# A spectral layer and an MLP in one kernel: x over the hardware queues, the first MLP block in two halves, the weight conversion on VectorE alone

## The chip, the cores and the metric

The kernel runs on one core of a Trainium2 chip. The metric is the device time of one execution in microseconds (us); the median of several runs counts. The core has a matrix engine (TensorE, PE in the profile, with its weight loads as PEld), VectorE (DVE), ScalarE (ACT), GpSimd (POOL) and SyncE (SP, which here only issues transfers). ACT, POOL and SP issue DMAs. Each engine works through its own instructions in order, and waits on semaphores for the others.

## The reference

```
X = rfft(x, axis=1)                       # x: 4 x 3008 x 256 float32
Yr = Xr @ w_r - Xi @ w_i + b_r
Yi = Xr @ w_i + Xi @ w_r + b_i
Y  = shrink(Yr, 0.01) + 1j * shrink(Yi, 0.01)     # sign(v) * max(|v| - 0.01, 0)
y  = irfft(Y, n=3008, axis=1)             # 4 x 3008 x 256
h  = y.reshape(12032, 256) @ moe_w_in     # moe_w_in: 256 x 2048, float64
out = (h * sigmoid(h)) @ moe_w_out        # moe_w_out: 2048 x 256, float64
```

## The kernel before, in words

The transform of length 3008 is done in two steps of products with tables, 47 x 64. For each of the four batches b, x is cut into eight groups g of 4 columns j (94 partitions x 1024 floats, 4 KB in a row).

- **s1** (one g): two products of 512 columns with table c1 into PSUM, a copy by ACT (tile s1o), and a store to a scratch tensor scr1 in DRAM.
- **The u loop**, twelve steps: u_load reads two rows of scr1 (tile a), **s2** multiplies with c2, ACT and DVE split the result into a high and a low part (xh, xl), **mix** multiplies with w_r and w_i in 24 products, DVE adds the bias and shrinks (y, three instructions), **split_z** makes zh and zl of y, **i1** multiplies with table c3 (tile t3) in six products, and ACT copies and stores the result to scr2.
- **i2**: reads scr2 (tile gin) and finishes the inverse transform for one block of 512 tokens, split into a high and a low part again (xt). i2_ends does the columns that cross a block's end.
- **The MLP**: 24 blocks of 512 tokens (the last has 256), 16 slices f of the hidden size each. One pair (block, f) is a **tick**: mlp1 (six products of 512 columns), sigmoid on ACT, the product g on DVE (L474), gh on ACT, gl on DVE (L484), and two ticks later mlp2 (per 128 tokens one product of 512 and one of 256 columns), which adds up in four PSUM banks (acc) over all 16 f.

A product of plain float32 runs as two passes on PE; a float32r one is one pass, and so three of them (high x high, high x low, low x high) stand for one exact product.

The weights of the MLP come as float64. Sixteen pieces (eight of w_in, eight of w_out; four for each quarter of f) are converted by w64_split: first an ACT instruction, then with one w_go the first half (L560, L561 on DVE), with the next w_go the second half (L566, L567 on DVE, L569 on ACT, L570 and L571 on POOL). w_begin loads the next piece and starts one.

The order is written out by hand: each engine's instructions stand in the order of the code. Ahead of the ticks (the prologue) come s1 of b = 0, the u loop of b = 0 with half a weight in most steps, s1 of b = 1, and i2 of block 0. From then on the list `ticks` sets the order, and `fill` says what stands behind mlp1 of which tick: i2 of the blocks ahead, weights (W_PLAN), and the transform of the other batches.

x loads go through POOL's queue (L149). b = 0's u loop takes its y split by POOL (L358). Loads and most stores go through SP, stores of scr2 in the u loop through ACT.

Of the kernel before, what the change touches and what calls it, by code (L numbers as in the profile page):

```python
# [21 lines left out]
NU = NR // 2  # L22
# [10 lines left out]
X_BUFS = [0, 1, 2, 3, 4, 5, 6, 0, 1, 2, 3, 4, 5, 2, 1, 0]  # L33
# [3 lines left out]
def dft_tables():  # L37
# [16 lines left out]
    for h in range(2):  # L54
# [33 lines left out]
    c3l = c3 - c3h  # L88
    return {
# [3 lines left out]
        "c4": c4.reshape(96, NP).astype(np.float32),  # L93
    }
# [3 lines left out]
def spectral_mlp_kernel(ctx: ExitStack, tc: tile.TileContext, x, w_r, w_i, b_r, b_i, w_in, w_out, c1, c2, c3, c4, out):  # L98
# [44 lines left out]
    def x_load(b, g):  # L143
        if b < 2:
            t = x_pre[X_BUFS[8 * b + g]]
        else:
            t = x_sb[g % 2]
        v = x[b].rearrange("(p j) d -> p (j d)", j=NJ)
        nc.gpsimd.dma_start(out=t[:NP, :], in_=v[:, g * 4 * D:(g + 1) * 4 * D])  # L149
        return t  # L150
# [15 lines left out]
    def s1(b, g, late=False):  # L166
        t = x_t.pop((b, g))
        if b == 1 and g > 4:
            o = x_pre[(4, 6, 2)[g - 5]][:96, :]
        else:  # L170
            tag, bufs = ("s1o", 2) if 8 * b + g in (6, 7, 10, 11, 12) else ("gin", 4)
            o = sb.tile([128, 4 * D], F32, tag=tag, bufs=bufs, name="s1o")[:96, :]
# [180 lines left out]
    def split_z(b, u):  # L353
# [135 lines left out]
    def mlp2(i, f):  # L489
        n = BLOCKS[i][1]  # L490
        gh, gl = gf.pop((i, f))
        for t in range(n // 128):
            if f == 0:
# [3 lines left out]
            if i == LAST:  # L497
# [8 lines left out]
                start=(f == 0), stop=False,  # L506
# [3 lines left out]
                start=False, stop=(f == NFF - 1),  # L510
# [36 lines left out]
    def w64_split(t, shape, hi, lo):  # L547
# [3 lines left out]
        def shaped(a):  # L551
# [10 lines left out]
                                       op0=ALU.bitwise_and, op1=ALU.bitwise_or)  # L562
        yield
# [5 lines left out]
        nc.scalar.copy(hi, w)  # L569
        nc.gpsimd.tensor_sub(w, w, hi)  # L570
        nc.gpsimd.tensor_tensor(out=lo, in0=w, in1=shaped(lw), op=ALU.add)  # L571

    with tc.manual_schedule():
# [72 lines left out]
        def u_step(b, u):  # L646
            if u < NU:
                if u + (3 if b == 0 else 2) < NU:
                    u_load(b, u + (3 if b == 0 else 2))
                s2(b, u)  # L650
            if u > 0:
                t3_load(b, u - 1)
            if b == 0:
                if u > 2:
                    w_go()
                if u % 2:
                    w_begin()
            if 0 <= u - 2 < NU:
                split_z(b, u - 2)
            if 0 <= u - 1 < NU:  # L660
                mix(b, u - 1)
            if 0 <= u - 3 < NU:
                i1(b, u - 3)
# [6 lines left out]
        w32 = [w_load(w_r), w_load(w_i)]  # L670
# [9 lines left out]
        for u in range(NU):  # L680
            u_step(0, u)
# [3 lines left out]
            if 1 < u < 8:  # L685
# [3 lines left out]
        split_z(0, NU - 2)  # L689
        t3_load(0, NU - 1)  # L690
        mix(0, NU - 1)
        i1(0, NU - 3)
        s1(1, 2)
        split_z(0, NU - 1)
        i1(0, NU - 2)
        w_tags[:] = [(("y", 2), ("i1o", 2)), (("zl", 2), ("zh", 2))]
        s1(1, 3, late=True)
# [4 lines left out]
        i2_load(0)
        flush(1)
        for g in (4, 5, 6, 7):
            s1(1, g, late=True)
            w_go()
            if g == 5:
                w_begin()
            if g > 5:
                w_go()  # L710
# [12 lines left out]
        taken = set(range(17, len(ticks), NFF))  # L723
# [9 lines left out]
        for i in range(1, len(BLOCKS)):  # L733
            at(16 * i - 9, i2_load, i)
            put(16 * i - 7, i2, i, 0)
            put(16 * i - 5, i2, i, 1)
            put(16 * i - 3, i2_ends, i)
        for t, (go, begin) in enumerate(W_PLAN):
            for _ in range(go):
                at(t, w_go)  # L740
            for _ in range(begin):
                at(t, w_begin)
        for t in (10, 11):
# [12 lines left out]
        for b, t0, dt in ((2, 30, 7), (3, 110, 8)):  # L756
# [49 lines left out]
```

## Time and profile before

| | us |
|---|---|
| median of 3 runs | 1387.65 (1385.81 to 1388.34) |
| profiled execution, time | 1388.13 |
| profiled execution, span | 1386.3 |
| PE busy in it | 1364.3 |
| DVE busy | 898.2 |
| ACT busy | 711.2 |
| POOL busy | 170.0 |

The span runs from the first to the last instruction; the execution's own time is 1.8 us longer. Busy time counts a slow instruction in full, so PE's share says little about how close it is to dense work.

### The profile page before, as it was taken

Reading aid. Unit: us, or ns where it says so; the run is one execution under the profiler, and the core shown is the slowest. Engines: PE = TensorE matmul, PEld = TensorE weight load, DVE = VectorE, ACT = ScalarE, POOL = GpSimd, SP = SyncE. Lnnn points to the kernel's source line nnn. Section 1 sums busy time; section 2 is a strip of 40 time slices with the busy share of each in tenths; the row PEclk is TensorE's granted clock in tenths of the full one; section 3 lists DMA queues with packets and bytes.
Section 4 is the critical chain, followed back from the end, with each engine's and each line's share of the span. In section 5 each row is a group of like instructions: output and inputs, shape, how many; then the busy total and the mean of one; then the engine's idle time right before and its main releaser. Section 6 shows DMA issues by size and latency. Waiting matters only on the chain.

```text
span 1386.3 us, 20474 instructions
## 1 busy us (share of the span) xinstructions
PE 1364.3 (98%) x7638; PEld 1169.3 (84%) x7638; DVE 898.2 (65%) x1485; ACT 711.2 (51%) x1394; POOL 170.0 (12%) x205
## 2 busy tenths in 40 slices
PE   7998999999999999999999999999999999999998
PEld 3976788888888888888888888888888888888888
DVE  3899868777655677767655577776654555455555
ACT  5565555555554555555454445455444444444444
POOL 2555411120100011111100011111000000000000
PEclk9999999999999999999999999999999999999999
DMA  8975232331423214233121121220210110011001
GB/s 250 318 230 172 76 100 83 96 92 42 124 76 85 58 35 114 69 114 80 46 77 41 33 76 51 84 81 24 61 27 16 27 39 9 19 27 39 1 16 24
DMA packets 69855, 105.09 MB, mean 76 GB/s; under 512 B 7228, under 2 KB 51388, under 8 KB 69756
## 3 DMA queue, kind: packets, MB, share of 16 engines
q1 hardware_dynamic: 55685, 75.18, 18.5%
q0 software_dynamic: 10496, 24.91, 7.1%
q10 hardware_dynamic: 3575, 3.70, 0.8%
q8 instruction: 60, 0.98, 0.3%
q14 instruction: 39, 0.32, 0.1%
HBM read 66.28 MB, written 37.49 MB: 75 GB/s over the span
## 4 chain that ended last, share of the span: by engine, by line
PE 89%; DVE 4%; DMA 3%; issue 2%; ACT 1%; POOL 0%; ACTq 0%; SPq 0%; DVEq 0%; POOLq 0%
PE h L466 36%; PE acc L504 24%; PE acc L508 12%; PE mix L324 6%; PE i L410 3%; PE s L299 2%; PE i L368 2%; PE s L164 2%; PE acc L499 1%; DVE ww L560 1%; PE mix L263 1%; DMA scr<-i1o 1%; PE i2e L410 1%; DMA x_pre<-in_x_dram 1%; DVE gl L484 1%
## 5 line engine op out<-in xcount | busy, mean ns | idle before, releaser
L466 PE MATMUL h<-xt,win 128*128 128x512 f32 (+1 forms) x2304 | 588.5, 391 | 1.8 <-ACT xt L443 1.6
L504 PE MATMUL acc<-wout,gh 128*128 128x512 f32 x1472 | 540.0, 401 | 0.0
L466 PEld LDWEIGHTS h<-xt,win 128*128 128x128 f32 x2304 | 403.4, 189 | 85.3 <-ACT xt L443 1.7
L473 ACT ACTIVATE g<-h 128x512 f32<-128x512 f32 (+1 forms) x385 | 226.5, 588 | 387.6 <-PE h L466 386.3
L474 DVE TENSOR_TENSOR g<-h,g 128x512 f32<-128x512 f32 (+1 forms) x385 | 261.4, 679 | 242.2 <-ACT g L473 238.9
L508 PE MATMUL acc<-wout,gl 128*128 128x256 f32 x1472 | 413.0, 281 | 4.8 <-DVE gl L484 4.8
L484 DVE TENSOR_TENSOR gl<-g,gh 128x512 fp32r<-128x512 f32 (+1 forms) x385 | 282.1, 733 | 174.8 <-ACT gh L483 170.4
L504 PEld LDWEIGHTS acc<-wout,gh 128*128 128x128 f32 x1472 | 277.4, 188 | 59.0
L483 ACT CAST gh<-g 128x512 fp32r<-128x512 f32 (+1 forms) x385 | 235.1, 611 | 156.0 <-DVE g L474 153.6
L508 PEld LDWEIGHTS acc<-wout,gl 128*128 128x128 f32 x1472 | 278.6, 189 | 16.1 <-DVE gl L484 7.2
L331 POOL TENSOR_TENSOR q<-q,bias 128x256 f32<-128x256 f32 x36 | 26.4, 733 | 672.7 <-ACT q L330 672.7
L344 DVE TENSOR_TENSOR y<-q,mix 64x256 f32<-64x256 f32 x144 | 60.3, 419 | 2.2
L410 PEld LDWEIGHTS i<-c_sb,gin 96*128 96x128 f32 x420 | 54.4, 191 | 6.6 <-issue 1.7
L410 PE MATMUL i<-c_sb,gin 96*128 96x94 f32 x420 | 53.9, 272 | 1.6 <-DMA gin<-scr 1.6
L368 PE MATMUL i<-zh,t 128*128 128x256 f32 x192 | 45.4, 298 | 0.0
L299 PEld LDWEIGHTS s<-t,a 128*128 128x128 f32 x288 | 37.7, 191 | 3.0
L299 PE MATMUL s<-t,a 128*128 128x128 f32 x288 | 37.9, 274 | 0.0
L164 PE MATMUL s<-sx,c 94*96 94x512 f32 (+1 forms) x120 | 35.5, 404 | 1.0 <-DVE sx L195 0.3
L368 PEld LDWEIGHTS i<-zh,t 128*128 128x128 f32 x192 | 33.1, 190 | 1.1 <-issue 0.5
L520 DVE TENSOR_TENSOR o<-acc,o 128x256 f32<-128x256 f32 x92 | 32.4, 415 | 0.0
L332 POOL TENSOR_TENSOR q<-q,bias 128x256 f32<-128x256 f32 x36 | 32.0, 888 | 2.8
L426 DVE TENSOR_TENSOR xt<-i,xt 128x376 fp32r<-128x376 f32 (+2 forms) x48 | 28.0, 584 | 6.1 <-ACT xt L425 6.0
(113 smaller groups left out, 1232.3 us busy)
## 6 DMA issues: line engine op xcount, KB each, us to landing
a<-scr SPq DMA_DIRECT2D x48, 256.0 KB
t<-in_c_dram POOLq DMA_DIRECT2D x48, 256.0 KB, 3.2
gin<-scr SPq DMA_DIRECT2D x32, 384.0 KB
scr<-s1o SPq DMA_DIRECT2D x28, 384.0 KB
x_sb<-in_x_dram POOLq DMA_DIRECT2D x25, 376.0 KB, 4.4
scr<-i1o SPq DMA_DIRECT2D x36, 256.0 KB
t<-in_c_dram SPq DMA_DIRECT2D x48, 128.0 KB
w<-in_moe_w_in_dram SPq DMA_DIRECT2D x8, 512.0 KB
```

Source lines behind the costliest of these rows:

```text
L164: nc.tensor.matmul(out=p[:96, :], lhsT=c1_hl[m][:K, :], rhs=hl[k][:K, :], start=(n == 0), stop=(n == 2))
L299: nc.tensor.matmul(out=pv[:, e, :, r, :], lhsT=a[:, r, e * 128:(e + 1) * 128], rhs=t2[:, r * 128:(r + 1) * 128], start=True, stop=True,)
L324: nc.tensor.matmul(out=out, lhsT=x_[:, e, c, :], rhs=m[:, e, :], start=(n == 0), stop=(n == 5))
L368: nc.tensor.matmul(out=pv[:, r, :], lhsT=t3[:, m, r * 128:(r + 1) * 128], rhs=z[:, r, :], start=(n == 0), stop=(n == 2),)
L410: nc.tensor.matmul(out=p[:, o:o + m], lhsT=g_t[b, j // 4][:, q:q + 128], rhs=c4_sb[:, p0:p0 + m], start=True, stop=True,)
L466: nc.tensor.matmul(out=p[:, :n], lhsT=w[:, e, f * 128:(f + 1) * 128], rhs=v[:, e, :n], start=(m == 0), stop=(m == 5),)
L473: nc.scalar.activation(out=g[:, q], in_=p[:, q], func=ACTF.Sigmoid)
L474: nc.vector.tensor_tensor(out=g[:, q], in0=p[:, q], in1=g[:, q], op=ALU.mult)
L483: nc.scalar.copy(gh[:, q], g[:, q])
L484: nc.vector.tensor_sub(gl[:, q], g[:, q], gh[:, q])
L504: nc.tensor.matmul(out=a, lhsT=gh[:, q], rhs=wout[:, f].rearrange("p a c -> p (a c)"), start=(f == 0), stop=False,)
L508: nc.tensor.matmul(out=a[:, D:2 * D], lhsT=gl[:, q], rhs=wout[:, f, 0, :], start=False, stop=(f == NFF - 1),)
```

## The change

1. **x of b = 0 by the hardware queues.** Each of the eight loads is cut in two: 64 partitions on SP, 30 on ACT (the last one on SP as well). POOL and DVE zero the unused partitions; ACT no longer does. Loads of b = 1 stay on POOL.
2. **s1 of b = 0**: the second half of each g from 2 to 7 is split into high and low parts, the first half is a float32 product; before, both halves of g = 4 to 7 were split. w_r and w_i are loaded behind s1 of g = 5.
3. **i1 of b = 0 in float32**, straight from y: split_z goes, c3 comes as one float32 table (c3f) over SP.
4. **Weight conversion**: L570 and L571 move from POOL to DVE; ACT's copy of the high part comes half a step earlier.
5. **Block 0 in halves of f**: ticks are block 0 with f 0 to 7, block 1 with all f, block 0 with f 8 to 15, and then as before. The sums of the first half are kept in x_sb[1] and added at the end. So the pieces for f 8 to 15 are needed eight ticks later; W_GO and W_BEGIN spread the sixteen remaining halves over 20 ticks. s1 of b = 1, g = 5 to 7, moves from the prologue into the ticks 0 to 8 (s1_later); i2 of block 1 comes at ticks 1, 3 and 5. The tiles xt get four names (a and b) for their two generations.

```diff
-W_PLAN = [(1, 1), (1, 1), (1, 0), (2, 1), (1, 1), (1, 0), (1, 1), (3, 1), (0, 0), (1, 0), (1, 1), (2, 0), (1, 0)]
-
-S1_SPLIT = (4, 5, 6, 7)
+W_GO = (0, 1, 3, 4, 6, 7, 8, 9, 10, 12, 13, 14, 15, 17, 18, 19, 20, 21, 22)
+W_BEGIN = (1, 4, 7, 9, 12, 14, 17, 19)
+
+S1_SPLIT = (2, 3, 4, 5, 6, 7)
...
+        if b == 0:
+            nc.sync.dma_start(out=t[:64, :], in_=v[:64])
+            (nc.scalar if g < 7 else nc.sync).dma_start(out=t[64:NP, :], in_=v[64:])
+        else:
+            nc.gpsimd.dma_start(out=t[:NP, :], in_=v)
...
-            if b == 0 and g in S1_SPLIT:
-                k, w, n = ("x", 768, 2) if (2 * g + i) % 5 > 2 else ("g", 512, 3)
+            if b == 0 and g in S1_SPLIT and i:
+                k, w, n = ("x", 768, 2) if g % 2 else ("g", 512, 3)
...
+    def s1_later(g, i):
+
+        t = x_t[1, g]
+        if i == 0:
+            x_t[1, g, "o"] = sb.tile([128, 4 * D], F32, tag="s1o", bufs=2, name="s1o")[:96, :]
+        o = x_t[1, g, "o"]
+        p = bank("s1")
+        q = slice(i * 512, (i + 1) * 512)
+        nc.tensor.matmul(out=p[:96, :], lhsT=c1_sb, rhs=t[:, q], start=True, stop=True)
+        nc.scalar.copy(o[:, q], p[:96, :])
...
+        if b == 0:
+            t3_t[b, u] = sb.tile([128, 256], F32, tag="t3", bufs=5, name="t3f")
+            nc.sync.dma_start(out=t3_t[b, u], in_=c3f[:, u * 256:(u + 1) * 256])
+            return
...
+            if b == 0:
+                nc.tensor.matmul(out=pv[:, r, :], lhsT=t3[:, q], rhs=z[:, r, :], start=True, stop=True)
+                continue
...
-        if f == NFF - 1:
+        if ends:
             for t in range(n // 128):
                 a = acc.pop((i, t))
+                half = x_sb[1][:, t * D:(t + 1) * D]
+                if f == 7:
+                    nc.scalar.copy(half, a[:, D:2 * D])
+                    nc.vector.tensor_tensor(out=half, in0=a[:, 0:D], in1=half, op=ALU.add)
+                    continue
...
+                if i == 0:
+                    nc.vector.tensor_add(o, o, half)
...
+        nc.scalar.copy(hi, shaped(w.bitcast(F32)))
         yield
...
-        nc.scalar.copy(hi, w)
-        nc.gpsimd.tensor_sub(w, w, hi)
-        nc.gpsimd.tensor_tensor(out=lo, in0=w, in1=shaped(lw), op=ALU.add)
+        nc.vector.tensor_sub(w, w, hi)
+        nc.vector.tensor_tensor(out=lo, in0=w, in1=shaped(lw), op=ALU.add)
...
-            if n % 2:
-                nc.scalar.memzero(t[64:128, :])
-            else:
-                nc.vector.memset(t[64:128, :], 0.0)
+            (nc.gpsimd if n % 2 else nc.vector).memset(t[64:128, :], 0.0)
...
-        ticks = [(i, f) for i in range(len(BLOCKS)) for f in range(NFF)]
+
+        ticks = [(0, f) for f in range(8)] + [(1, f) for f in range(NFF)] + [(0, f) for f in range(8, NFF)]
+        ticks += [(i, f) for i in range(2, len(BLOCKS)) for f in range(NFF)]
...
+        for g in (5, 6, 7):
+            for i in range(2):
+                t = put(0, s1_later, g, i)
+            if g == 5:
+                at(t, x_ahead)
```

What this does to the order is to be seen in three places. First the start. Before, POOL's queue has all x loads, in this order (x_sb and x_pre are the tiles of x):

```order
L582 MEMSET zero 128x512
L149 DMA x_sb_69<-in_x_dram 94x1024
L149 DMA x_sb_70<-in_x_dram 94x1024
L149 DMA x_sb_96<-in_x_dram 94x1024
L149 DMA x_pre<-in_x_dram 94x1024 x4
```

In the changed kernel SP has the larger halves, ahead of the stores of s1 (scr_0); the rows name in brackets what each waits for (DMAHW is the landing of an earlier transfer of SP or ACT):

```order
L617 DMA c_sb<-in_c_dram 128x96
L154 DMA x_sb_69<-in_x_dram 64x1024
L154 DMA x_sb_70<-in_x_dram 64x1024
L154 DMA x_sb_96<-in_x_dram 64x1024
L154 DMA x_pre<-in_x_dram 64x1024
L154 DMA x_pre<-in_x_dram 64x1024 [waits DMAHW1_49]
L154 DMA x_pre<-in_x_dram 64x1024 [waits DMAHW3_49]
L154 DMA x_pre<-in_x_dram 64x1024 [waits DMAHW5_49]
L250 DMA t_131<-in_c_dram 128x256 [waits DMAHW7_49]
L192 DMA scr_0_82<-s1o 96x1024 [waits DMAHW0_49,Activation_49]
```

The loads moved from a queue of their own to the queue of the stores, and from the fifth on each waits for the landing of an earlier one. ACT issues the other halves before its first copy.

Second, DVE in the u loop, in a step with the second half of a weight (we, ww: the weight's tiles; xl, y, c: those of the loop). Before:

```order
L250 TENSOR_TENSOR xl<-s_605,xh 128x4x128
L566 TENSOR_SCALAR we<-ww 128x512
L567 SCALAR_TENSOR_TENSOR we<-w_311,we 128x512
L270 TENSOR_TENSOR y<-mix,bias 128x512
L271 TENSOR_SCALAR c<-y 128x512
L272 TENSOR_TENSOR y<-y,c 128x512
```

and after:

```order
L274 TENSOR_TENSOR xl<-s_525,xh 128x4x128
L603 TENSOR_SCALAR we<-ww 128x512
L604 SCALAR_TENSOR_TENSOR we<-w_339,we 128x512
L606 TENSOR_TENSOR ww<-ww,win_79 128x512
L607 TENSOR_TENSOR win_80<-ww,we 128x512
L294 TENSOR_TENSOR y<-mix,bias 128x512
```

Two instructions more stand on DVE between xl and y; POOL, which had them (L570, L571) and one zl (L358) in each step, has only x loads left there.

Third, PE from the last i1 of b = 0 to the first mlp1 (i_: i1, then i2; s_: s1; h: mlp1). Before:

```order
L368 MATMUL i_1075<-zh,t_998 128x256
L183 MATMUL s_1097<-x_pre,c_sb 96x512
L183 MATMUL s_1100<-x_pre,c_sb 96x512
L183 MATMUL s_1109<-x_sb_96,c_sb 96x512
L183 MATMUL s_1112<-x_sb_96,c_sb 96x512
L183 MATMUL s_1121<-x_sb_70,c_sb 96x512
L183 MATMUL s_1124<-x_sb_70,c_sb 96x512
L183 MATMUL s_1135<-x_sb_69,c_sb 96x512
L183 MATMUL s_1138<-x_sb_69,c_sb 96x512
L410 MATMUL i_1149<-c_sb,gin 128x94 x5
L410 MATMUL i2e<-c_sb,gin 128x94 x2
```

and after:

```order
L393 MATMUL i_983<-y,t3f 128x256 x2
L188 MATMUL s_994<-x_pre,c_sb 96x512
L188 MATMUL s_997<-x_pre,c_sb 96x512
L188 MATMUL s_1005<-x_sb_69,c_sb 96x512
L188 MATMUL s_1008<-x_sb_69,c_sb 96x512
L437 MATMUL i_1023<-c_sb,gin 128x94 x5
L437 MATMUL i2e<-c_sb,gin 128x94 x2
L437 MATMUL i_1041<-c_sb,gin 128x94 x5
```

Four s1 products instead of eight stand between the last i1 and i2, which reads what that i1 wrote by way of scr2. The others stand behind mlp1 in the ticks.

## Rows read from the trace of the kernel before

**Rows 1.** Stretches: width, busy time of PE, PEld, DVE, ACT, POOL, clock, DMA, GB/s

```profile
31.74:39.60 7.86, 7.57 (x41) 7.31 (x41) 1.38 (x2) 2.58 (x6) 1.39 (x3) 0.62 0.96 295
39.60:88.78 49.18, 48.23 (x401) 47.29 (x399) 46.28 (x61) 28.57 (x60) 33.29 (x34) 1.00 1.03 297
88.78:101.44 12.66, 12.66 (x44) 5.93 (x42) 10.57 (x13) 10.01 (x19) 5.32 (x4) 1.00 0.53 154
101.44:107.67 6.23, 3.27 (x25) 2.83 (x25) 5.99 (x8) 2.79 (x6) 3.60 (x4) 1.00 0.58 193
107.67:161.07 53.40, 48.07 (x214) 38.22 (x215) 49.62 (x66) 26.55 (x49) 29.37 (x21) 0.90 0.47 143
```

**Rows 2.** Chain that ended last, in order of time: start, us, what

```profile
39.76 0.89 PE s L242 x8
40.66 2.89 PE mix L263 x24
...
88.94 0.72 PE i L368 x6
89.66 1.72 PE s L183 x4
...
179.01 1.39 PE h L466 x6
181.79 1.39 PE h L466 x6
```

**Rows 3.** Instructions in order of time, DVE in the u loop: start, us, what

```profile
40.60 0.43 DVE L271 TENSOR_SCALAR c<-y 128x512 f32<-128x512 f32 x1
41.06 0.69 DVE L272 TENSOR_TENSOR y<-y,c 128x512 f32<-128x512 f32 x1
...
48.34 1.48 DVE L271 TENSOR_SCALAR c<-y 128x512 f32<-128x512 f32 x1
```

**Rows 4.** The same of POOL, at the third of those rows

```profile
48.27 1.28 POOL L358 TENSOR_TENSOR zl<-y,zh 128x512 fp32r<-128x512 f32 x1 [2.19 <-ACT zh L357]
```

**Rows 5.** Groups by line and form, 0 to 165 us: count, busy us, mean ns

```profile
L560 DVE TENSOR_SCALAR ww<-ww 128x512 uint32<-128x512 uint32 x16 | 16.1, 1004 | 0.0
L561 DVE SCALAR_TENSOR_TENSOR ww<-w,ww 128x512 uint32<-128x512 uint32 x16 | 15.8, 989 | 0.5
```

**Rows 6.** In order of time, PE in tick 5, with the wait before it

```profile
125.52 0.38 PE L508 MATMUL acc<-wout,gl 128*128 128x256 f32 x1 [2.31 <-DVE gl L484]
```

**Rows 7.** In order of time, ACT's queue and PE, 96 to 108 us

```profile
96.11 0.37 ACTq L135 DMA_DIRECT2D scr<-i1o  x1
...
102.43 1.10 PE L410 MATMUL i<-c_sb,gin 96*128 96x94 f32 x8 [0.85 <-DMA gin<-scr]
...
104.36 0.61 PE L410 MATMUL i2e<-c_sb,gin 96*128 96x94 f32 x4
104.81 1.28 PE L410 MATMUL i<-c_sb,gin 96*128 96x94 f32 x10
107.67 1.24 PE L466 MATMUL h<-xt,win 128*128 128x512 f32 x3 [1.58 <-ACT xt L443]
```

**Rows 8.** DMA by queue, stretches 6 to 14, 18 to 22 and 373.4 to 378.2 us

```profile
q0 software_dynamic: 549, 1.89, 99.8%
...
DMA packets 469, 1.62 MB, mean 405 GB/s; under 512 B 74, under 2 KB 74, under 8 KB 469
...
DMA packets 332, 1.15 MB, mean 240 GB/s; under 512 B 51, under 2 KB 51, under 8 KB 332
```

**Rows 9.** In order of time, the queues, ACT and PE at the start

```profile
0.74 0.42 SPq L581 DMA_DIRECT2D c_sb<-in_c_dram  x1
2.25 0.69 POOL L149 DMA_DIRECT2D x_sb<-in_x_dram  x1 [0.94 <-DVE x_sb L587]
10.73 13.86 SPq L187 DMA_DIRECT2D scr<-s1o  x8
...
19.41 1.07 ACT L184 COPY s1o<-s 96x512 f32<-96x512 f32 x2 [3.33 <-DMA scr<-s1o]
...
31.74 2.05 PE L242 MATMUL s<-t,a 128*128 128x128 f32 x8 [4.99 <-DMA a<-scr]
```

More of the change, by code (lines that the diff above doesn't have):

```diff
@@ L93, in dft_tables, with spectral_mlp_kernel @@
         "c4": c4.reshape(96, NP).astype(np.float32),
+        "c3f": c3f,
     }
 @with_exitstack
-def spectral_mlp_kernel(ctx: ExitStack, tc: tile.TileContext, x, w_r, w_i, b_r, b_i, w_in, w_out, c1, c2, c3, c4, out):
+def spectral_mlp_kernel(ctx: ExitStack, tc: tile.TileContext, x, w_r, w_i, b_r, b_i, w_in, w_out, c1, c2, c3, c4, c3f, out):
     nc = tc.nc
@@ L189, in s1 @@
             store(v[:, g * 4 * D:(g + 1) * 4 * D], o, late)
+    def s1_later(g, i):
[7 more added lines that the diff above has]
+        nc.scalar.copy(o[:, q], p[:96, :])
+        if i:
+            v = scr1[1].rearrange("r (a j) d -> (r a) (j d)", a=4)
+            store(v[:, g * 4 * D:(g + 1) * 4 * D], o)
+            del x_t[1, g], x_t[1, g, "o"]
     def s1_split(b, g, i):
@@ L417, in i2 @@
         if e == 0:
-            xt[i] = tuple(sb.tile([128, 2, BLK], F32R, tag=f"xt{k}", bufs=2, name=f"xt{k}") for k in range(2))
+            v = "ab"[i > 0] if i < 3 else "ab"[(i + 1) % 2]
+            xt[i] = tuple(sb.tile([128, 2, BLK], F32R, tag=f"xt{v}{k}", bufs=1, name=f"xt{k}") for k in range(2))
         whole = [v for v in pieces(c0, n) if v[4] == NP]
@@ L536, in w64_load @@
     def w64_load(src):
-        tag, bufs = ("s1o", 2) if len(weights) < 6 and len(weights) % 3 else ("gin", 4)
-        t = sb.tile([128, 512, 2], U32, tag=tag, bufs=bufs, name="w64")
+        t = sb.tile([128, 512, 2], U32, tag="gin", bufs=4, name="w64")
         out = t.rearrange("p n two -> p (n two)")
@@ L643, in u3_step, with u_step @@
                 mix3(b, u - 1)
-        def u_step(b, u):
+        def u_step(u):
             if u < NU:
[L648 to L657, printed above, removed]
-            if 0 <= u - 2 < NU:
[L659 to L663, printed above, removed]
+                if u + 3 < NU:
+                    u_load(0, u + 3)
+                t3_load(0, u)
+                s2(0, u)
+            if u > 1:
+                w_go()
+            if 0 <= u - 1 < NU:
+                mix(0, u - 1)
+            if u % 2 and u < NU:
+                w_begin()
+            if 0 <= u - 2 < NU:
+                i1(0, u - 2)
         t2_load(0, 0)
@@ L669, in spectral_mlp_kernel @@
                 x_ahead()
-        w32 = [w_load(w_r), w_load(w_i)]
+            if g == 5:
+                w32 = [w_load(w_r), w_load(w_i)]
         u_load(0, 0)
@@ L688, in spectral_mlp_kernel @@
                 nc.sync.dma_start(out=c4_sb, in_=c4)
[L689 to L692, printed above, removed]
+        w_begin()
+        u_step(NU)
         s1(1, 2)
[L694 to L697, printed above, removed]
+        flush(1)
+        u_step(NU + 1)
+        i2_load(0)
+        w_tags[:] = [(("zl", 2), ("zh", 2))]
+        s1(1, 3)
         w_go()
-        i1(0, NU - 1)
+        flush(1)
+        s1(1, 4)
         w_go()
         w_begin()
[L702 to L710, printed above, removed]
         i2(0, 0)
         i2_ends(0)
+        w_go()
         i2(0, 1)
+        i2_load(1)
+        w_go()
         w_begin()
+        flush(1)
         state["prologue"] = False
-        ticks = [(i, f) for i in range(len(BLOCKS)) for f in range(NFF)]
+        ticks = [(0, f) for f in range(8)] + [(1, f) for f in range(NFF)] + [(0, f) for f in range(8, NFF)]
+        ticks += [(i, f) for i in range(2, len(BLOCKS)) for f in range(NFF)]
         fill = {}
@@ L721, in at @@
             fill.setdefault(t, []).append((fn, args))
-        taken = set(range(17, len(ticks), NFF))
+        taken = {9, 25} | set(range(33, len(ticks), NFF))
         def put(t, fn, *args):
@@ L733, in spectral_mlp_kernel @@
         for i in range(1, len(BLOCKS)):
[L734 to L743, printed above, removed]
+            t = 16 * i - 9 if i > 1 else -1
+            if i > 1:
+                at(t, i2_load, i)
+            put(t + 2, i2, i, 0)
+            put(t + 4, i2, i, 1)
+            put(t + 6, i2_ends, i)
+        for t in W_GO:
+            at(t, w_go)
+        for t in W_BEGIN:
+            at(t, w_begin)
+        for g in (5, 6, 7):
+            for i in range(2):
+                t = put(0, s1_later, g, i)
+            if g == 5:
+                at(t, x_ahead)
+        for t in (11, 35):
             at(t, x_ahead)
```

39 lines of the change are left out of this document (19 added, 20 removed).

## Prediction

> **What bounds the kernel now.** I read the stretches first, then the chain of work, then VectorE beside GpSimd. TensorE (PE) is busy almost everywhere, so the question is where it does less than it could. That needs a price for dense work. From the chain [rows 2]: s2 of one u takes 0.89 us, its mix 2.89, its i1 0.72, one s1 of 1024 columns in plain float32 1.72 (four passes of 512 columns, 0.43 each), and mlp1 of one tick 1.39. Two mlp1 start 2.78 us apart where nothing is in the way, so mlp2 has the other 1.39. An i2 instruction takes 0.11 (four between 104.36 and 104.81 in [rows 7]).
>
> With these prices I compare work and width of each stretch [rows 1]:
> - 31.74 to 39.60: two s2 and a mix, 4.7 us of work in 7.9, at a granted clock of 0.62. PE had waited 4.99 us for the first load of scr1 [rows 9]. 3.2 lost.
> - 39.60 to 88.78, the loop over u: ten s2, eleven mix, nine i1 are 8.9 + 31.8 + 6.5 = 47.2 in 49.2. 2.0 lost.
> - 88.78 to 101.44: three i1 and six s1, 12.5 in 12.7. 0.2 lost.
> - 101.44 to 107.67, i2 of block 0: 24 instructions, 2.7 in 6.2. 3.5 lost.
> - 107.67 to 161.07, the first ticks: 15 mlp1 and 13 mlp2 (38.9) and 20 i2 instructions (2.2), 41.1 in 53.4, clock 0.90. 12.3 lost.
>
> From 161 on ticks follow each other densely. So all that can be won lies in the first 161 us: 21.2 us there and whatever the start holds. The reader is to see that "busy" is the wrong measure (48.07 of 53.40), because a busy row can be a slow one.
>
> What holds PE in the first ticks is VectorE (DVE): PE waits 2.31 us for one gl of L484 [rows 6]. And DVE is late because its instructions are long. Alone, a TENSOR_SCALAR takes 0.43 and a two-input subtract 0.69; with GpSimd (POOL) at work the same TENSOR_SCALAR takes 1.48 [rows 3], and POOL was running its zl subtract at that moment [rows 4]. Over the first 165 us the two weight instructions L560 and L561 average 1.00 and 0.99 [rows 5], against 0.43 and 0.69 alone.
>
> **The start.** The seven x loads of b = 0 begin when POOL has waited for a memset, at 2.25 [rows 9]. Moved to SP, the first one follows c1 (issued at 0.74), so about 1.1 us earlier. The seven loads are 94 x 4 KB each, 2.7 MB; between 6 and 14 us the software queue alone fills the DMA engines with 1.89 MB in 8 us [rows 8], 237 GB/s. A store of scr1 issued at 10.73 puts nothing on its queue in that stretch (99.8% is the software queue's), and ScalarE (ACT) then waits 3.33 us, until 19.41, for a store to land and free its buffer [rows 9]. So stores begin when the loads have drained, and everything up to the first s2 shifts with the loads. Against that, from the fifth half load on SP and ACT wait for the landing of an earlier load, and ACT, which now issues seven half loads, is held until the third x has landed, about 8 us; it had nothing to copy before 8.4 anyway. The loads of w_r and w_i now go ahead of the last two stores instead of behind them; they were between the last store and the first load of scr1 in either order, and the first load of scr1 no longer stands behind their packets. I take -1.5 for the start. Bounds: if the x loads ran at the 405 GB/s of the stretch with both queues in use [rows 8], 2.7 MB would take 6.7 instead of 11.4, and the gain would be about 5; if the waits between loads leave gaps, +1.
>
> A hardware queue with the same shape of load (gin: 96 pieces of 4 KB) moves 240 GB/s in a later stretch of its own [rows 8], so I don't take the 405. A rule bears on this: the Trainium skill, DMA: Bandwidth & Descriptors, section "Issuing engines are not separate DMA queues", says that DMAs from any engine run on the same 16 DMA engines and that using several issuers only saves the issuing time. By the rule the start gains that 1 us or so; by the 405 row it would gain 5.
>
> **The loop over u.** Removed: twelve casts on ACT (L357), ten subtracts on POOL and two on DVE (L358). i1 of b = 0 becomes two float32 products per u instead of six of the fast kind: each is two passes of 256 columns, at half the price of a 512-column pass, so 4 x 0.215 = 0.86 against 0.72, and 12 x 0.14 = +1.7 on PE. Bounds for it: 0 (no dearer than the six) and +7 (a pass of 256 columns at 0.33, between half and all of a 512-column one). In return i1 no longer waits for zl, which POOL made: the 2.0 lost in the loop and the 0.2 behind it go, -2.2.
>
> DVE must then not become the bound. Per u it has xl 0.69, y 0.69 + 0.43 + 0.69, and in turn the first half of a weight (0.43 + 0.69) or the second, now with both POOL instructions (0.43 + 0.69 + 0.69 + 0.69): 3.6 and 5.0, mean 4.3, against 0.89 + 2.89 + 0.86 = 4.64 on PE. It fits, if the instructions keep their lone lengths; POOL has only x loads to issue then. t3 at half the bytes, on SP, lightens DMA engines that are full in this stretch (share 1.03 in [rows 1]).
>
> **From the last i1 to dense ticks.** Before, five s1 lay about and behind the last i1; now three go to the ticks. I time the new order from the end of the last i1 (call it E). ACT copies (0.6), issues the store; from a store's issue to the first i2 takes 96.11 to 102.43 = 6.3 [rows 7], so i2 starts at E + 7.0, while PE has only two s1 (3.4) to do: 3.6 idle. The second gin costs another 0.9, i2 of e = 0 ends at E + 9, ACT and DVE convert it by E + 10.5 and the first three mlp1 products run; ACT's copy of a weight waits for DVE's first half (1.1) and stands before the second i2's cast, so mlp1 of tick 0 ends at E + 13.6. Then the order on PE: s1 half 14.5, mlp1 15.9, i2 of block 1 (its gin issued at about E + 11, landed by E + 15) 16.8, mlp1 18.2, s1 half 19.1, mlp2 20.5, mlp1 21.9. The work in it is 3.4 + 2.7 + 4 x 1.39 + 1.7 + 0.9 + 1.4 = 15.7, so 6.2 lost.
>
> Later ticks: DVE has g and gl (0.69 each) and, in 16 of the first 20 ticks, half a weight (3.6 over two). Over 20 ticks 27.6 + 29.0 = 56.6, against 20 x 2.78 on PE plus six s1 halves (5.2) and i2 of block 1 (2.2) = 63. PE is the bound again: the weights of f 8 to 15 are needed from tick 16 instead of tick 8. Where the second half of a weight stands before the saving of block 0's half (tick 9), mlp2 of the next tick waits for its accumulators: DVE needs 1.3 + 2.5 + 4 x 0.4 behind mlp1, PE comes back after 2.8, so about 1.1 lost, and 0.8 more for the like. The slow clock after PE's gap: before, 0.90 over 53 us means some 10 us at the lower of two levels (1.2 against 2.4 GHz), 5 us of work lost; one gap instead of several, I take 2.5 (bounds 0 and 6). Together 6.2 + 1.9 + 2.5 = 10.6 lost, against 3.5 + 12.3 = 15.8 before: -5.2. The six s1 halves are the same work in another place. The four additions of block 0's saved half are DVE work of 0.4 each beside dense PE work; uncovered they would cost 1.6.
>
> **Sum.** -1.5 - 2.2 + 1.7 - 5.2 = -7.2. The profiled execution took 1388.1 us (span 1386.3 and 1.8 around it), 0.5 above the median of the runs: 1388.1 - 7.2 = 1380.9, and I say 1381.
>
> **The rivals.**
> - *The start gains more* (hardware queues carry x at 405 GB/s): 4 us more, 1377. For it speaks the high rate once both kinds of queue are in use; against it the 240 GB/s of the lone gin loads [rows 8].
> - *The gap eats the gain.* Behind the last i1 PE is idle for 3.6 us and works little for another 6, and only then do ticks start with work that is spread thin. If the clock stays at its lower level through the first four or five ticks, 10 to 12 us of work run at half speed, 5 to 6 lost rather than 2.5, and the half weights delay gl by a tick more: -7 becomes -2, 1386, no change that can be told. For it: the clock of 0.62 after a wait of 5 us [rows 1, 9]. Against it: before, the same place was disturbed as well.
> - *Slower: VectorE becomes the bound.* If its instructions stay long for another reason than POOL, a u costs it 0.69 + 0.69 + 1.0 + 1.0 + half of (1.0 + 1.0 + 1.0 + 3 x 1.0) = 6.4 by the means of [rows 5], 1.7 more than PE's 4.64, so +17 over ten u, and the ticks win nothing: about 1400. It decides where DVE needs more than 4.64 per u. Against it: every lone row is short [rows 3].
>
> **How the numbers follow.** About 0.2% (2.8 us) is what a measurement of this kernel tells from no change: below 1384.9 counts as faster. The sum as it stands (1378 to 1384.5) 0.50; more at the start 0.15; the gap eats the gain 0.24, of which 0.06 still lies below 1384.9 and 0.18 within 0.2%; VectorE as the bound, or another new wait, 0.11. Faster 0.50 + 0.15 + 0.06 = 0.71, same 0.18, slower 0.11. The range that leaves 2 in 10 out: 1375.5 to 1387; the likeliest case's own is 1378 to 1384.5.
>
> **What would show it.** Right: the weight instructions on DVE at 0.43 and 0.69 throughout; i1 at 0.86 with no wait before it; first s2 at about 30 us; PE dense from about tick 4 on; no PE wait on gl over 1 us. Wrong: a first s2 after 32, a wait on y or xl in the loop over u, a PE wait at gin of over 5 us, a clock below 0.9 beyond tick 5.

## The result, and the profile after

Before 1387.94 us (median of 4 runs), after 1400.04 (1399.22 to 1401.34, 4 runs): ratio 1.0096, interval 1.0083 to 1.0108. The kernel became 0.96% slower where 0.5% faster was forecast, and the time lies 13 us above the range.

The stretches of the changed kernel, as in [rows 1]: two s2 and the first mix; the loop over u; the last two i1 with three s1; i2 of block 0; ticks 0 to 14; the ticks up to mlp1 of tick 37.

```profile
32.63:46.55 13.92, 8.29 (x40) 8.03 (x41) 1.39 (x2) 2.58 (x6) 0.51 (x2) 0.53 1.02 273
46.55:98.40 51.85, 50.28 (x386) 48.44 (x385) 42.50 (x74) 25.24 (x52) 0.00 (x0) 1.00 0.71 225
98.40:105.63 7.23, 7.20 (x21) 3.29 (x20) 6.96 (x13) 4.46 (x9) 0.00 (x0) 1.00 0.41 131
105.63:117.45 11.82, 5.35 (x25) 5.21 (x25) 3.33 (x7) 2.91 (x8) 0.52 (x1) 0.70 0.67 207
117.45:169.27 51.82, 48.25 (x228) 38.04 (x228) 40.34 (x72) 27.10 (x56) 0.52 (x1) 0.97 0.38 114
169.27:253.45 84.18, 79.87 (x459) 68.57 (x457) 66.64 (x116) 43.83 (x91) 15.28 (x19) 1.00 0.33 93
```

Two s2 and a mix took 7.86 us before and take 13.92 at a clock of 0.53; i2 with its wait took 6.23 and takes 11.82. The last stretch is the one to notice: before, the ticks that led to the same mlp1 (161.07 to 240.49) had no idle PE at all, 79.42 busy in 79.42; now 4.3 us are idle.

Times of the same work in both profiles give a ledger. First s2: 31.74 before, 32.63 after, +0.9. End of the last i1 (E, as in the prediction; read at the start of the product behind it): 94.56 and 102.20, +7.6, although one s1 less (1.72) stands ahead of it now. Mlp1 of tick 37: 240.49 and 253.45, +13.0. From there on the distance stays (+13.3 at the end). By the forecast the three would have read -1.5, -3.7 (-1.5 - 2.2 + 1.7, and that s1) and -7.2.

**The first place: the loads of POOL.** In order of time, POOL of the changed kernel, then PE:

```profile
30.57 1.04 POOL L157 DMA_DIRECT2D x_pre<-in_x_dram  x2
31.61 1.53 POOL L157 DMA_DIRECT2D x_sb<-in_x_dram  x3
106.09 0.52 POOL L157 DMA_DIRECT2D x_sb<-in_x_dram  x1 [72.95 <-PE s L188]
...
32.63 2.05 PE L266 MATMUL s<-t,a 128*128 128x128 f32 x8 [5.06 <-issue]
40.31 2.05 PE L266 MATMUL s<-t,a 128*128 128x128 f32 x8 [5.63 <-DMA a<-scr]
```

POOL of the kernel before, at the same work:

```profile
43.76 1.28 POOL L358 TENSOR_TENSOR zl<-y,zh 128x512 fp32r<-128x512 f32 x1 [10.64 <-ACT zh L357]
44.99 0.55 POOL L149 DMA_DIRECT2D x_pre<-in_x_dram  x1
...
48.27 1.28 POOL L358 TENSOR_TENSOR zl<-y,zh 128x512 fp32r<-128x512 f32 x1 [2.19 <-ACT zh L357]
49.50 0.55 POOL L149 DMA_DIRECT2D x_pre<-in_x_dram  x1
```

Before, each x load of batch 1 stood behind a zl (L358) that waits for the y of its step, so there was one load per u. Without zl nothing in POOL's order holds them, and all five loads (376 KB each) leave within 2.6 us, just when the first rows of scr1 are wanted. DMA in 32 to 40 us, changed kernel, then before:

```profile
q0 software_dynamic: 421, 1.48, 70.6%
q1 hardware_dynamic: 602, 0.55, 26.2%
```

```profile
q1 hardware_dynamic: 1401, 1.92, 77.2%
q0 software_dynamic: 288, 0.52, 21.0%
```

The hardware queue, which carries scr1, gets 0.55 MB through instead of 1.92, and the second s2 waits 5.63 us for its tile a. Part of that is that SP asked for less: its load of a weight, which left at 34.74 before, was held for 4.0 us until an a had landed (L578) and left at 40.24. That so few bytes remain fits the Trainium skill, DMA: Bandwidth & Descriptors, section "Queues, rings and completion order", by which each DMA engine takes the queues that it has work for in turn, a packet at a time: here 421 packets of some 3.5 KB stand against 602 of 0.9 KB. No run takes the two parts apart.

**The second place: a copy on ACT.** Waits of the changed kernel, 108 to 200 us: who waited for whom, us in total, times, longest; of ACT, DVE and PE:

```profile
ACT wout L599 <- DVE ww L597: 15.0, 5, 5.2
ACT win L599 <- DVE ww L597: 11.4, 4, 4.2
...
DVE gl L512 <- ACT gh L511: 12.9, 12, 1.7
...
PE acc L534 <- DVE x_sb L548: 3.6, 1, 3.6
PE acc L538 <- DVE gl L512: 2.9, 3, 2.2
```

ACT waits 26.4 us in nine waits for the first half of a weight on DVE, because its copy of the high part (L599) now stands in the same half step. What that does is seen at the half save, in order of time:

```profile
150.16 0.69 DVE L597 SCALAR_TENSOR_TENSOR ww<-w,ww 128x512 uint32<-128x512 uint32 x1
150.89 0.62 ACT L599 CAST wout<-ww 128x512 fp32r<-128x512 f32 x1 [3.48 <-DVE ww L597]
...
151.89 0.62 ACT L511 CAST gh<-g 128x512 fp32r<-128x512 f32 x1
...
152.54 0.69 DVE L512 TENSOR_TENSOR gl<-g,gh 128x512 fp32r<-128x512 f32 x1 [1.69 <-ACT gh L511]
...
156.14 1.41 DVE L548 TENSOR_TENSOR x_sb<-acc,x_sb 128x256 f32<-128x256 f32 x4
156.61 0.50 PE L534 MATMUL acc<-wout,gh 128*128 128x512 f32 x1 [3.57 <-DVE x_sb L548]
```

ACT stands still for 3.48 us with gh behind it; DVE has nothing to do for 1.69 until gh is there, and comes late to the second half and the save. PE pays 3.57.

**Two smaller places.** Behind the last i1, stores of s1 on ACT's queue, then SP, and PE:

```profile
104.73 0.33 ACTq L139 DMA_DIRECT2D scr<-s1o  x1
106.71 0.33 ACTq L139 DMA_DIRECT2D scr<-s1o  x1
...
106.00 1.02 SPq L408 DMA_DIRECT2D gin<-scr  x2
...
102.20 1.88 PE L188 MATMUL s<-x_pre,c_sb 128*96 128x512 f32 x4
...
112.26 2.50 PE L437 MATMUL i<-c_sb,gin 96*128 96x94 f32 x10 [6.47 <-issue]
```

i2 starts at E + 10.06 (forecast 7.0; before 7.87, from 94.56 to the 102.43 of [rows 7]). Beside gin there are two stores of s1 on ACT's queue and POOL's load at 106.09, which left early too; e7 below tests whether they make the difference. And at tick 15:

```profile
170.90 2.74 POOL L311 TENSOR_TENSOR w32d<-w 128x512 f32<-128x512 f32 x2 [22.61 <-DMA bias<-in_b_r_dram]
171.36 1.13 DVE L603 TENSOR_SCALAR we<-ww 128x512 uint32<-128x512 uint32 x1
172.52 1.67 DVE L604 SCALAR_TENSOR_TENSOR we<-w,we 128x512 f32<-128x512 uint32 x1
...
176.17 0.39 PE L538 MATMUL acc<-wout,gl 128*128 128x256 f32 x1 [2.22 <-DVE gl L512]
```

While POOL makes w32d, DVE's two instructions take 1.13 and 1.67 instead of 0.42 and 0.69, and PE waits 2.22 for gl.

### The profile page after: what moved, and what is told of

It is laid out like the page before. It is cut to its first block, busy times and chain, and to the rows that moved or that the text cites. A ratio compares the mean times of both kernels' runs of the same rounds, so it can differ in the third digit from the quotient of the medians.

```text
span 1399.6 us, 20366 instructions
## 1 busy us (share of the span) xinstructions
PE 1363.6 (97%) x7612; PEld 1170.1 (84%) x7612; DVE 887.7 (63%) x1519; ACT 700.3 (50%) x1383; POOL 99.6 (7%) x146
## 4 chain that ended last, share of the span: by engine, by line
PE 92%; DVE 3%; DMA 2%; ACT 1%; issue 1%; SPq 0%; ACTq 0%; DVEq 0%
PE h L494 36%; PE acc L534 24%; PE acc L538 12%; PE mix L348 6%; PE i L437 3%; PE mix L287 2%; PE s L323 2%; PE i L396 2%; PE s L172 2%; DMA scr<-s1o 1%; PE acc L529 1%; PE s L266 1%; DVE gl L512 1%; PE i L393 1%; DMA a<-scr 1%
## 5 line engine op out<-in xcount | busy, mean ns | idle before, releaser
L512 DVE TENSOR_TENSOR gl<-g,gh 128x512 fp32r<-128x512 f32 (+1 forms) x385 | 276.1, 717 | 182.8 <-ACT gh L511 176.3
L355 POOL TENSOR_TENSOR q<-q,bias 128x256 f32<-128x256 f32 x36 | 26.4, 733 | 671.9 <-ACT q L354 664.6
L396 PE MATMUL i<-zh,t 128*128 128x256 f32 x144 | 33.7, 297 | 1.4 <-issue 1.4
L453 ACT CAST xt<-i 128x376 fp32r<-128x376 f32 (+2 forms) x48 | 24.1, 503 | 20.3 <-PE i L437 20.3
```

Source lines behind the costliest of these rows:

```text
L396: nc.tensor.matmul(out=pv[:, r, :], lhsT=t3[:, m, q], rhs=z[k][:, r, :], start=(n == 0), stop=(n == 2),)
L512: nc.vector.tensor_sub(gl[:, q], g[:, q], gh[:, q])
```

## The experiments

Eighteen kernels, each timed against the kernel before on the same chip. Medians in us, ratio to before with its interval:

| kernel | built on | median | ratio |
|---|---|---|---|
| e1 paced | after | 1397.0 | 1.0070 (1.0058 to 1.0083) |
| e2 burst | before | 1396.25 | 1.0067 (1.0055 to 1.0080) |
| e3 x on POOL | after | 1400.69 | 1.0102 (1.0088 to 1.0116) |
| e4 half moved | after | 1398.01 | 1.0078 (1.0065 to 1.0092) |
| e5 paced, same addresses | after | 1394.69 | 1.0054 (1.0041 to 1.0066) |
| e6 w32d on DVE | e5 | 1393.52 | 1.0044 (1.0032 to 1.0057) |
| e7 tail | e5 | 1392.46 | 1.0036 (1.0023 to 1.0048) |
| e9 unused tile | after | 1400.34 | 1.0094 (1.0078 to 1.0109) |
| e8 part 4 alone | before | 1389.23 | 1.0017 (1.0008 to 1.0026) |
| e11 w behind s1 | e5 | 1393.48 | 1.0044 (1.0032 to 1.0057) |
| e13 copy late | e5 | 1388.09 | 1.0006 (0.9997 to 1.0015) |
| e14 four edits | e5 | 1383.01 | 0.9970 (0.9959 to 0.9982) |
| e15 five edits | e14 | 1381.51 | 0.9960 (0.9948 to 0.9973) |
| e16 copy late alone | after | 1394.12 | 1.0053 (1.0040 to 1.0065) |
| e17 copy early | before | 1403.82 | 1.0122 (1.0107 to 1.0138) |
| e18 tile again | e5 | 1396.77 | 1.0069 (1.0056 to 1.0081) |
| e19 split as before | e15 | 1380.89 | 0.9955 (0.9942 to 0.9968) |
| e20 start as before | e15 | 1381.02 | 0.9957 (0.9943 to 0.9970) |

**The burst: e1, e2, e5.** Theory A: the burst of x loads costs the time; rival B: the loads cost the same wherever they lie. e1, in the loop over u of the changed kernel:

```diff
+        pace = cst.tile([128, 1], F32, name="pace")
...
             if 2 < u < 8:
+                nc.gpsimd.tensor_copy(out=pace, in_=u_t[0, u - 1][:, 0, 0:1])
                 x_ahead()
```

> The changed kernel, with one more POOL instruction ahead of each of the five x loads of batch 1 in the u loop: it copies one number per partition of the newest y, so that a load is issued once per u, at about 45 to 65 us, instead of all five between 30.6 and 33.1. Theory A (the loads come in a burst because POOL lost the zl work that had paced it, and hold up the first loads of scr1): the second s2 starts near 36 instead of 40.3, the last i1 ends near 96.5 instead of 102.2, and the time falls by 5 to 6.5 us to 1393.5 to 1395. Rival B (the DMA engines have the same bytes to move in any order, and the loss lies in the start or on VectorE): the second s2 stays at 39 to 40, and the time within 1.5 us of 1400.

e2, in the kernel before:

```diff
+        for _ in range(6):
+            x_ahead()
         for u in range(NU):
             u_step(0, u)
...
-            if 1 < u < 8:
-                x_ahead()
```

> The kernel before, with its six x loads of batch 1 written ahead of the u loop instead of one per step in it; nothing else. Theory A: a burst at about 30 us as in the changed kernel, the second s2 comes 4 to 5 us later, time 1392 to 1394 (+4 to +6). Rival B: within 1 us of 1388.

e2 is 9 us slower than before, more than A asked for. The wait that A looked for comes, though at the fourth s2 instead of the second. POOL and PE, in order of time:

```profile
30.24 1.54 POOL L149 DMA_DIRECT2D x_pre<-in_x_dram  x3
31.78 1.52 POOL L149 DMA_DIRECT2D x_sb<-in_x_dram  x3
...
30.04 3.79 PE L242 MATMUL s<-t,a 128*128 128x128 f32 x16 [3.77 <-DMA a<-scr]
46.49 2.04 PE L242 MATMUL s<-t,a 128*128 128x128 f32 x8 [5.30 <-DMA a<-scr]
```

B falls. Most of the rest of the 9 us is the slower clock behind the wait: the granted clock is 0.65 from 46.49 to 60.00, which by estimate costs 4.7 of those 13.5 us, where the kernel before has 1.00 from its fourth s2 (43.37) to 60. In e1 the last i1 ended at 94.29, 7.9 us earlier than in the changed kernel, but the time fell by 3 only. From mlp1 of tick 40 to the last mlp1 it took 1128.32, the changed kernel 1126.07: 2.2 lost, a little at a time (the 3.3 in the next expectation is too much). So e5 has the same edit with the tile in a place that existed already (tag "rest").

> The paced kernel again, but the one-column tile that POOL writes now lies in a place that was there already, so that no other tile's address moves. In the first paced run the last i1 came 7.9 us earlier (as theory A wants, even more), but the ticks from 400 us on then lost 3.3 us little by little, 0.2%, with products of 229 to 236 ns in another rhythm. Theory D (the new tile moved all tiles behind it by a few bytes, and that changed the rhythm): the drift goes, 1393 to 1394.5. Rival (the drift comes from POOL's five copies or from the new order of the loads): 1396.5 to 1397.5, the ticks drift as before.

e5 has no drift and wins 5.4 us; its first two s2 follow each other without a wait:

```profile
32.49 3.76 PE L266 MATMUL s<-t,a 128*128 128x128 f32 x16 [5.27 <-issue]
39.98 1.06 PE L266 MATMUL s<-t,a 128*128 128x128 f32 x8
```

At the last i1 (94.34) its profile shows 7.9 won, of which 2.2 are lost again up to tick 37. Between e16 and e13 below, which both have ACT's copy late, the same edit wins 6.0.

**The drift: e9, e18.** e9 adds `unused = cst.tile([128, 1], F32)` behind c4_sb in the changed kernel, e18 adds it to e5 where e1 had its tile, as the last of the pool of constants.

> The changed kernel with one tile of 128 partitions x 1 float32 more in the pool of constants, which nothing reads or writes. Theory D: every tile behind it moves by its size, the ticks lose about 0.2% from 250 us on, 1402.5 to 1404. Rival: no instruction is added, so within 0.7 us of 1400.

> The paced kernel with the same addresses (e5, 1394.7) and a tile of one column more in the pool of constants at the place in the code where the first paced kernel (e1) had it; nothing reads or writes it. If that tile's place made the drift of e1: the ticks from 250 us on lose 0.2%, 1397 to 1398. Rival (the drift came from what POOL wrote there, or from the execution): within 0.7 us of 1394.7, ticks as in e5.

e9 changes nothing in the time; e18 is 2.1 slower and drifts like e1. Mlp1 of tick 40 and of one of the last ticks, e5, then e18:

```profile
260.66 1.55 PE L494 MATMUL h<-xt,win 128*128 128x512 f32 x6
...
1376.63 0.89 PE L494 MATMUL h<-xt,win 128*128 128x256 f32 x6
```

```profile
258.97 1.56 PE L494 MATMUL h<-xt,win 128*128 128x512 f32 x6
...
1377.42 0.86 PE L494 MATMUL h<-xt,win 128*128 128x256 f32 x6
```

1115.97 us in the one, 1118.45 in the other, for the same instructions. The medians of e5 and e18 have intervals that overlap, but the stretch from mlp1 of tick 40 to the last mlp1 tells the kernels apart: 1126.04 to 1126.16 in the changed kernel and every one built on it except three, 1128.32 in both e1 and e18, and 1126.65 in e9. So a tile that nobody touches costs 0.2% if it lies last among the constants, and a quarter of that where e9 has it, too little to show in the median. The loss is not the same everywhere: up to the last block e18 loses 2.7, and in that block, of 256 tokens, it gains 0.4.

**The copy: e13, e16, e17.** e13 on e5, and e16 on the changed kernel, put ACT's copy back where it was; e17 moves it early in the kernel before.

```diff
-        nc.scalar.copy(hi, shaped(w.bitcast(F32)))
         yield
...
         w = shaped(w.bitcast(F32))
+        nc.scalar.copy(hi, w)
         nc.vector.tensor_sub(w, w, hi)
```

> The paced kernel with the same addresses (e5), with ACT's copy of a weight's high part (L599) back in the second half, behind L604 in the order, as it was before the change. Theory H (in the ticks ACT waits 26 us in nine waits at L599 for VectorE's L597 of the same tick, and gh and the sigmoid stand behind it, so VectorE in its turn waits for gh and comes late to the half save): these waits go, PE's wait for x_sb falls from about 3.5 to 1 to 2, and 1.5 to 3 us are won: 1391.7 to 1393.2. Rival: VectorE then waits for the copy, which stands behind ACT's other work, and loses as much: within 0.7 us of 1394.7.

> The changed kernel with ACT's copy of the high part back in the second half, and nothing else; the x loads of batch 1 still come in a burst. If the two causes act apart: 1400 - 6.6 = 1393.4, between 1392.5 and 1394.5, with the second s2 still at about 40 us. If the late start of the loop over u hides part of it (or the other way about): 1395.5 to 1398.

> The kernel before with ACT's copy of the high part (L569) half a step earlier, behind L561, as the change has it; the second half's subtract and sum stay on POOL. If the place of the copy costs by itself (ACT waits for VectorE's L561 with the sigmoid and gh behind it): 1390 to 1393. Rival (it costs only where VectorE has the second half too): 1386.5 to 1388.5.

e13 wins 6.6 us, e16 5.9, e17 loses 16.6. In e13 the waits of ACT at the copy are gone from 108 to 200 us, and PE's waits there are 2.4 us in all:

```profile
PE acc L534 <- DVE x_sb L548: 1.4, 1, 1.4
PE acc L538 <- DVE gl L512: 1.0, 1, 1.0
```

In e17 (32 to 165 us) ACT waits 35.7 us at the copy, and PE for gh, which it never did before, and longer for POOL's zl:

```profile
ACT win L563 <- DVE ww L561: 18.3, 8, 3.8
ACT wout L563 <- DVE ww L561: 17.4, 7, 5.0
...
PE acc L504 <- ACT gh L483: 8.6, 4, 3.7
...
PE i L368 <- POOL zl L358: 6.2, 5, 1.8
```

Theory H holds, at more than twice the size that I gave it, and the copy and the burst act apart. That e17 loses more than the changed kernel has one cause in these rows: zl waits for zh, which stands behind the copy on ACT, and PE waits 6.2 us for zl in the loop over u (0.9 before), while the changed kernel has no zl. Its longer L561 (0.99 [rows 5]), for which ACT waits, may add to it; no run shows how much.

**Part 4's other half: e8.** `nc.gpsimd` becomes `nc.vector` in L570 and L571 of the kernel before.

> The kernel before with the two POOL instructions of a weight's second half (L570, L571) on DVE, and nothing else of the change. Theory G (VectorE's long instructions come from POOL at work, and gl is late for that reason): L560 and L561 fall from 1.00 and 0.99 to near 0.43 and 0.69, the two PE waits of 2.4 us on gl go, 1383 to 1385.5. Rival (in these ticks one to three halves stand in each, so VectorE needs more than PE even with short instructions: 17 halves of 1.8 and 13 ticks of 1.4 are 49 us against some 43): the instructions are short and PE waits for gl as long or longer, 1387 to 1391.

1389.23, 2.3 slower: the rival. The instructions of the first half are shorter (1.00 and 0.99 before), L571 on DVE is not (POOL still makes zl in the loop):

```profile
L561 DVE SCALAR_TENSOR_TENSOR ww<-w,ww 128x512 uint32<-128x512 uint32 x16 | 12.0, 751 | 0.5
L571 DVE TENSOR_TENSOR wout<-ww,we 128x512 fp32r<-128x512 f32 x8 | 7.5, 940 | 0.3
L560 DVE TENSOR_SCALAR ww<-ww 128x512 uint32<-128x512 uint32 x16 | 6.7, 419 | 0.0
...
PE acc L508 <- DVE gl L484: 5.8, 5, 2.5
PE mix L263 <- DVE xl L250: 3.4, 3, 1.8
```

PE waits for gl 5.8 us instead of 4.8, and from the last i1 to mlp1 of tick 37 the two kernels take the same, 146.1 and 145.9. What e8 loses lies ahead of that, in the loop over u, where PE now waits 3.4 us for xl and never did before; its last i1 ends at 96.65 instead of 94.56. So shorter instructions won nothing in ticks that hold this many of them. That part 4 needs part 5, which spreads them, follows from it but was not measured.

**Smaller places: e4, e6, e7, e11.** e4 moves the halves of ticks 9 and 10:

```diff
-W_GO = (0, 1, 3, 4, 6, 7, 8, 9, 10, 12,
+W_GO = (0, 1, 3, 4, 6, 7, 8, 10, 11, 12,
```

> The changed kernel with the two weight halves of ticks 9 and 10 moved to ticks 10 and 11, so that none stands on VectorE between g of tick 9 and the saving of block 0's half. Theory: PE's wait of 3.6 us for x_sb (L548) falls to about 1, time 1397 to 1398 (-2 to -3). Rival: VectorE is short of time in these ticks anyway, and the wait comes back at gl one or two ticks later: 1399.5 to 1400.5.

2.0 us less; PE's wait for x_sb is 1.3 instead of 3.6. e6 has L311 on `nc.vector`:

> The paced kernel with the same addresses, and the two POOL instructions of mix3_weights that make the sum and the difference of w_r and w_i (L311, 2.74 us for both, at 170.9 in the changed kernel) on DVE. Theory E (at that moment VectorE's L603 and L604 took 1.13 and 1.67 instead of 0.42 and 0.69 because POOL was at work, gl came late and PE waited 2.2 us): the wait goes, 1.5 to 2.5 us less than the paced kernel. Rival: the two instructions cost VectorE 1.4 us in the same ticks, PE waits as long for gl: within 0.7 us of the paced kernel.

1.2 less than e5; the intervals overlap, so the median alone doesn't show it. From 155 to 185 us PE's waits for gl fell from one of 1.9 to three of 1.2 together. e7 gives s1(1, 2) to s1(1, 4) `late=True`, and POOL a copy of xt ahead of the load of x(1,7):

> The paced kernel with the same addresses, and two edits behind the last i1: the stores of s1 of batch 1, g 2 to 4, go from ACT's queue to SP's (late=True, as before the change), and POOL's load of x(1,7) waits for xt of block 0 by a copy of one column. Theory F (i2 starts 10 us instead of 7 us behind the last i1 because gin's packets share the DMA engines with stores on ACT's queue and a load on POOL's): i2 starts 7 to 8 us behind it, 2 to 3 us less than the paced kernel. Rival (a gin load takes so long from the landing of the last store on, whatever else moves): i2 at 9.5 to 10, within 0.7 us of the paced kernel.

2.2 less than e5, and i2 starts at 102.79, which is E + 7.87, as before the change, where e5 has E + 9.86. Which of the two edits does it was not taken apart. e11 loads w_r and w_i behind the loop over s1:

> The paced kernel with the same addresses (e5), with the loads of w_r and w_i behind the loop over s1, as before the change. Theory I (ahead of the last two stores of scr1 they hold these up, and with them the first s2): first s2 at 31 to 31.7 instead of 32.5, 0.8 to 1.5 us won. Rival (they lie between the same two things in either order, as the prediction had it): within 0.5 us of 1394.7.

1.2 less, the first s2 at 31.83; again the intervals overlap.

**Together: e14, e15.** e14 is e5 with e6, e7, e11 and e13; e15 has e4 as well.

> The paced kernel with the same addresses (e5, 1394.7) and four edits together: w32d on VectorE (alone -1.2), the tail's stores and load (alone -2.2), the copy of the high part late and w_r and w_i behind s1 (the two other kernels of this group). If the four act at places of their own, they add up: 1387 to 1389.5. If a gain at one place is given back at the next wait (the half save), 1390 to 1392.

> The kernel with four edits (e14, 1383.0; its PE still waits 1.4 us for x_sb at the half save) with the two halves of ticks 9 and 10 moved to 10 and 11 as well. If the wait goes: 1381.5 to 1382.2. If the halves only come to stand before another wait: 1382.6 to 1384.

The four add up (1394.7 - 1.2 - 2.2 - 1.2 - 6.6 = 1383.5; measured 1383.01), and e15 takes the half save's wait away too: from the last i1 to mlp1 of tick 37 it takes 141.6, e14 143.0, though the intervals of the two times overlap. Both beat both kernels: e15 is 0.4% below before.

**The start: e3, e19, e20.** e3 has x of batch 0 on POOL's queue again, e19 the split of s1 as before, e20 both.

> The changed kernel with part 1 undone: x of batch 0 by POOL's queue in one piece, as before. Theory A: the hardware queues carry x no faster than POOL's, so the start costs at most 1 us: first s2 at 31.5 to 32.6, time 1398.5 to 1400. Rival C (the start by the hardware queues is the cause of the loss, by later stores or by queues that stay full): the first s2 at 31 and the second by 36, time 1393 or less.

> The kernel with five edits (e15, 1381.5), with part 2 of the change undone in s1 of batch 0: both halves of g 4 to 7 split, instead of the second halves of g 2 to 7. If the split makes the start late: first s2 at 30 to 31, 1380 to 1380.7. Rival (the start is set by stores that wait for the x loads to drain): within 0.6 us of 1381.5.

> The same, and x of batch 0 by POOL's queue as well, so that the start is that of before but for the memsets. If x by the hardware queues makes the start late (ACT held in issues, two of x's eight loads late on SP), together with the split: first s2 at 29.6 to 31, 1379.5 to 1380.5. Rival (the order of executions: the start of before was itself late by 2 us in its one profile and early in others): within 0.6 us of 1381.5.

None makes a difference; with the start of before the first s2 comes at 33.12 (e3) and 32.17 (e20). The start of this change is worth nothing in either direction.

## Why the prediction was wrong

**The step that failed first** is "POOL has only x loads to issue then", written as a relief for DVE. It removed twelve subtracts from POOL's or DVE's order and never asked what stood behind POOL's ten: six x loads, which those subtracts had held to one per u. The price is 5.4 us (e5) to 6.0 (e16 to e13), and 9 in the kernel before (e2).

**The step that failed most** is the cost of part 4 and of the later ticks. I set DVE's 56.6 us against PE's 63 over 20 ticks and called PE the bound, and counted ACT's early copy once, 1.1 us in the tail. Sums of durations hide that ACT and DVE work in order and wait for each other: L599 waits for DVE, gh for L599, gl for gh. It cost 5.9 to 6.6 us (e16, e13), and moving two halves off the half save was worth 2.0 (e4). With the copy late, the sum's forecast for these ticks comes true: no wait on gl over 1 us, 1.4 at the half save (forecast 1.1).

**Mis-sized.** i2 at E + 7.0 was E + 10.06; 0.9 of that was in the kernel before already (7.87), where the store goes out 1.55 behind E (at 96.11 [rows 7]) and not 0.7. Without the stores and the load beside gin it is E + 7.87 (e7), the 2.2 us of that edit. That w_r and w_i "were between the last store and the first load of scr1 in either order" was off by perhaps 1.2 (e11). POOL's w32d beside DVE's weights was not in the sum: perhaps 1.2 (e6); that DVE is slower beside POOL was known from [rows 3], but I looked for POOL's work only where the change had removed it. The start at -1.5 measured 0 (e3, e20).

**Right.** x on hardware queues is no faster: 1.93 MB between 6 and 14 us after, 1.89 MB before [rows 8]. The weight instructions on DVE keep their lone lengths, 418, 692, 419, 693, 685 and 692 ns on average up to 165 us. In e5 the eight steps of the loop over u from 39.98 to 77.05 take 4.63 us each (forecast 4.64), so i1 in float32 and DVE's load were priced right; the ninth takes 5.42. The clock behind the gap lost little: 0.97 over ticks 0 to 14, 1.6 us by that (forecast 2.5).

**The rivals.** "VectorE becomes the bound, about 1400" gave the right time for a reason that did not hold: instructions stayed short. "Another new wait", put together with it at 0.11, is what happened, three times. My text named a first s2 after 32, a gap at gin over 5 us and a wait on y in the loop as signs against it; all three are in the profile after (32.63; 6.47; and 0.81 ahead of an i1 at 60.66, whose y was ready at 60.56). The first says little: e14, e19 and e20, which beat both kernels, have it too (32.32, 32.06, 32.17).

Put right, the change is worth about what was forecast: 1381.5 (e15) against 1381. That is not all its own merit, since e15 also moves w32d, which before did not do, and the agreement is in part luck. By stages e15 against before has the first s2 at +0.0 (31.77; forecast -1.5), the last i1 at -1.7 (92.86; forecast -3.7) and mlp1 of tick 37 at -6.0 (234.46; forecast -7.2). What stays open is why the place of an unused tile changes the pace of the ticks.

## What to carry to other kernels

When work is taken off an engine, list what else stands in that engine's order, its DMAs above all: the removed instruction may have been what held them back, and a transfer that leaves early competes with the one that is waited for. A copy of one column from the tile of the right step is enough to hold a load (0.18 us on POOL). And when an instruction is moved half a step earlier, ask for which engine it then waits and what stands behind it: a sum of busy times per engine says that work fits, not that it flows.

## What the runs showed of the hardware

An instruction of POOL with two inputs from SBUF slows DVE beside it, also an instruction with one input: L603 1.13 for 0.42, L604 1.67 for 0.69. By the Trainium skill, SBUF — State Buffer, section "Who interferes with whom", the two engines share a pair of ports that one holds for a whole instruction while the other is blocked. The page puts this on DVE instructions with two SBUF inputs and on the two-port modes of others. The rows agree for L604, which has two; in which mode L603 runs no run here shows.

I had not expected that the place of tiles changes the pace of PE at a granted clock of 1.00: 0.2% over 1116 us (e5 and e18), with the same instructions, and the same 1128.32 us in e1 and e18 on different chips. For a kernel that is tuned by fractions of a per cent, an edit that adds or drops a tile has to be measured against one that leaves the addresses alone.
